# Attention with routed FFN on one core: routing and FFN steps given out by other waiting times of the builder's model, another order behind the last output, a two-chain last FFN, and more warming matmuls

## The chip, the cores and the metric

The kernel runs on one core of one Trainium2 chip. The core has a matrix engine (PE, with its weight loads PEld), three engines for element work (DVE, ACT and POOL) and a queue engine (SP) that issues most DMAs. The metric is device microseconds of one execution; lower is better. Matrix sums are built in eight PSUM banks.

## What is computed

There are 8 batches of 3136 tokens with 256 features. Per batch, the reference computes squared-ReLU attention without a softmax, multiplies by `u`, and then lets the 128 tokens with the highest gate scores pass through a small FFN:

```python
scores = (1 / S) * z @ z.T              # z: 3136 x 64
x = u * (relu(scores) ** 2 @ v)         # v, u: 3136 x 256
s = x @ w_gate
top = argpartition(-s, 128)[:128]       # per batch
y = relu(x[top] @ w1) @ w2              # 256 -> 1024 -> 256
x[top] += sigmoid(s[top])[:, None] * y
```

The matrix products must keep nearly float32 accuracy, so the kernel splits operands into a high and a low part and multiplies hi·hi, hi·lo and lo·hi.

## The kernel before, in words

**Tiling.** A batch is cut into six chunks of 512 tokens (0 to 5; chunk 5 is called `FIFTH`) and a rest of 64 tokens (`WHOLE`). For each chunk the kernel goes over key tiles, two of 128 tokens at a time. One such pair is a *slot*. A slot has four score matmuls (`sc`, PE), the squared ReLU with its high and low part (`a`, `hi`, `lo`: ACT, DVE, POOL), and twelve product matmuls that add to the banks `acc` (PE). Squares that another chunk has computed already come back turned from DRAM (`qk<-squares`). When a chunk is complete, DVE evicts it times `u` (`ut<-acc,ut`), turns it and stores it to the output; POOL and DVE form its gate scores.

**Routing.** `route(b)` finds the 128th-highest score of a batch by radix search: eight rounds in which DVE counts (`ge`, `cnt`), PE sums over partitions (`tot`) and DVE settles four more bits. Then come `cols`, `places` and four `find` steps (`ids`), an indirect DMA that gathers the chosen rows from the output (`xe<-out,ids`, POOL queue), and the FFN (`expert`): `turn` (`xeT`), `hidden` (`h`), `turn_h` (`hT`), `back` (`y`). An indirect DMA (`scatter`) writes the rows back.

**The last batch.** Its rows are ranked in a first step over chunks 0 to 2; chunks 3 and 4 are merged in one at a time (`merge`), and chunk 5 and the rest together at the very end (`last_merge`, `finish_last`, `finish_rest`). The FFNs of the two batches before it are put off (`put_off`, the list `held`) and given out in the last slots, as filler behind the last attention work. So behind the last output there are: scores of chunk 5 and of the rest, counting on DVE, `find`, the gather, the last FFN and its scatter.

**What sets the order.** The order of instructions on every engine is fixed when the kernel is built. The builder keeps its own clock (`Clock`: a cost for every instruction, a time for every tile). Work that is not PE work is a `job` with a rank; PE work is chosen in `choices`: score matmuls first (priority 0), then steps of chains (1), then products (2 or 3), among those that are ready by the builder's clock. A *chain* is a list of steps on different engines, each started when the one before is done; routing and FFN are chains. `step_when` says when a chain's PE step may be given out: at its operands' time by the builder's clock plus `MARGIN` = 0.3 for chains with a negative `lag`, plus `FAR` = 1.5 for all others. On the chip nothing of this clock exists: an engine takes its instructions in the order given, and waits for semaphores. Where an operand is later on the chip than by the builder's clock, PE stands still, with all that is behind that instruction.

All batches' routing goes through one chain, `far`; the turning of `u` for the rest (`uT`) goes through it too. The put-off FFNs are two chains with lag 20, the last FFN and the rank search at the end are a chain with lag -9, and the rest's scores (`spread<-own`) are a chain with lag 0.

Constants (identity, tokens, gate weights) are loaded in an early slot by `load_consts`; one POOL job, `use_consts`, turns them and gives DVE five instructions with them. `start` begins with ten matmuls on zeros (`warm`) before the first data are there.

In the profile nearly every instruction has line L198, that of a helper which notes it; instructions are told apart by the names of their tiles.

## Time and profile before

| what | before |
|---|---|
| time, median of 3 runs | 2173.46 us (2173.14 to 2174.82) |
| the profiled execution's own time | 2174.97 us |
| its span, first to last instruction | 2173.2 us |
| PE busy | 2114.3 us (97%) |
| DVE, ACT, POOL busy | 65%, 63%, 62% |
| mean granted TensorE clock | 0.989 |
| DMA | 428 MB, 197 GB/s |

The time lies 1.8 us over the span. Rows of the timeline read: start in us, duration in us, engine, line, operation, out<-in, count; in brackets the idle time of the engine just ahead, and what ended it. In a list of waits the numbers are us in total, times, and the longest. In a table of windows, `PEclk` is the clock that TensorE was granted in that stretch, as a share of full speed.

### The profile page before, as it was taken

The numbers are of one execution on the slowest core, as the hardware profiler recorded it, in microseconds if no ns is written. First come the engines' busy times: TensorE is split into PE (matmuls) and PEld (weight loads), VectorE is DVE, ScalarE is ACT, GpSimd is POOL, SyncE is SP. The second block draws the span as 40 slices with busy tenths as digits, with TensorE's granted clock in tenths as the row PEclk, the third lists the DMA queues.
The fourth block names the chain that finished last, engine by engine and source line by source line (L and its number), as shares of the span: only waits on it lengthen the run. The fifth ranks groups of instructions, "written<-read, shape, count | busy, mean of one in ns | idle before, by whom it ended". The sixth has DMA issues, their size and how long they took to land. (4 is left out here: it accounts for less than half of the span.)

```text
span 2173.2 us, 29259 instructions
## 1 busy us (share of the span) xinstructions
PE 2114.3 (97%) x9558; PEld 1704.6 (78%) x9558; DVE 1420.2 (65%) x2156; ACT 1361.9 (63%) x1583; POOL 1350.9 (62%) x634
## 2 busy tenths in 40 slices
PE   8999999999999999999999999999999999999997
PEld 6788877888778887788877888778887887778775
DVE  6765587545975459754686556955579664876773
ACT  7676576655766557655676556666576665876542
POOL 6466666567755677556765568565785566756551
PEclk9999999999999999999999999999999999999998
DMA  6688867777686866877668777687776677658741
GB/s 195 200 244 236 202 194 203 216 203 183 194 224 201 214 171 192 245 217 189 180 202 245 203 189 192 198 245 190 182 214 187 190 190 193 202 168 232 179 119 64
DMA packets 426121, 428.38 MB, mean 197 GB/s; under 512 B 129008, under 2 KB 329328, under 8 KB 422384
## 3 DMA queue, kind: packets, MB, share of 16 engines
q1 hardware_dynamic: 424624, 423.89, 71.2%
q0 software_dynamic: 768, 2.10, 0.3%
q8 instruction: 75, 1.23, 0.2%
q14 instruction: 78, 0.64, 0.1%
q10 hardware_dynamic: 576, 0.52, 0.1%
HBM read 238.44 MB, written 175.37 MB: 190 GB/s over the span
## 5 line engine op out<-in xcount | busy, mean ns | idle before, releaser
L198 PE MATMUL acc<-hi,V 128*128 128x512 f32 x4800 | 1235.8, 395 | 8.5 <-DVE ut L198 5.8
L198 PEld LDWEIGHTS acc<-hi,V 128*128 128x128 f32 x4800 | 895.0, 189 | 206.2 <-DVE ut L198 7.1
L198 POOL TENSOR_TENSOR lo<-a,hi 128x1024 fp32r<-128x1024 f32 (+1 forms) x231 | 550.1, 2384 | 391.9 <-ACT a L198 238.2
L198 PE MATMUL acc<-lo,V 128*128 128x512 f32 x2304 | 640.8, 395 | 1.5 <-POOL lo L198 1.4
L198 DVE STREAM_TRANSPOSE aT<-a 128x512 f32<-128x512 f32 (+2 forms) x622 | 379.4, 646 | 274.1 <-ACT a L198 217.9
L198 PEld LDWEIGHTS acc<-lo,V 128*128 128x128 f32 x2304 | 432.4, 189 | 101.0 <-issue 5.4
L198 POOL TENSOR_TENSOR lo<-qk,hi 128x1024 fp32r<-128x1024 f32 x161 | 406.9, 2528 | 158.1 <-ACT hi L198 137.3
L198 ACT ACTIVATE a<-sc 128x1024 f32<-128x1024 f32 (+1 forms) x392 | 353.4, 902 | 226.9 <-DVE aT L198 114.0
L198 ACT ACTIVATE hi<-a 128x1024 fp32r<-128x1024 f32 (+1 forms) x384 | 366.4, 955 | 188.6 <-PE acc L198 182.4
L198 ACT CAST hi<-qk 128x1024 fp32r<-128x1024 f32 x240 | 251.8, 1049 | 241.1 <-PE acc L198 202.8
L198 PE MATMUL sc<-Z,ZH 128*128 128x512 f32 (+1 forms) x728 | 278.1, 385 | 9.7 <-ACT a L198 5.7
L198 PE MATMUL sc<-Z,ZL 128*128 128x512 f32 (+1 forms) x728 | 276.3, 382 | 0.3 <-POOL ZL L198 0.3
L198 ACT ACTIVATE a<-a 128x1024 f32<-128x1024 f32 x247 | 262.0, 1061 | 7.3
L198 DVE TENSOR_TENSOR lo<-a,hi 128x1024 fp32r<-128x1024 f32 (+1 forms) x105 | 186.2, 1774 | 43.9 <-ACT a L198 32.9
L198 DVE TENSOR_TENSOR a<-sc,a 64x512 f32<-64x512 f32 (+3 forms) x145 | 118.3, 816 | 91.4 <-ACT hi L198 70.7
L198 PEld LDWEIGHTS sc<-Z,ZH 128*128 128x128 f32 x728 | 137.9, 189 | 42.0 <-ACT a L198 8.6
L198 POOL TENSOR_TENSOR ut<-x,w_run 128x1024 f32<-128x1024 f32 x45 | 125.7, 2793 | 65.9 <-DVE x L198 65.9
L198 PEld LDWEIGHTS sc<-Z,ZL 128*128 128x128 f32 x728 | 139.0, 191 | 31.3 <-POOL ZL L198 0.8
L198 DVE TENSOR_TENSOR lo<-qk,hi 128x1024 fp32r<-128x1024 f32 x79 | 134.9, 1707 | 25.4 <-ACT hi L198 25.3
L198 DVE SCALAR_TENSOR_TENSOR ut<-acc,ut 128x512 f32<-128x512 f32 x96 | 62.6, 680 | 87.8 <-PE acc L198 87.7
L198 POOL TENSOR_TENSOR V<-vst,V 128x512 fp32r<-128x512 f32 x62 | 98.8, 1609 | 16.4 <-ACT V L198 12.8
L198 POOL TENSOR_TENSOR lo<-own,hi 128x512 fp32r<-128x512 f32 x47 | 63.5, 1351 | 65.3 <-ACT hi L198 53.4
(170 smaller groups left out, 1183.4 us busy)
## 6 DMA issues: line engine op xcount, KB each, us to landing
squares<-aT SPq DMA_DIRECT2D x240, 512.0 KB, 4.4
qk<-squares SPq DMA_DIRECT2D x480, 256.0 KB, 6.1
ut<-in_ut SPq DMA_DIRECT2D x48, 512.0 KB, 5.1
vst<-in_v SPq DMA_DIRECT2D x188, 128.0 KB, 3.7
out<-x SPq DMA_DIRECT2D x188, 128.0 KB, 3.5
squares_own<-aT SPq DMA_DIRECT2D x47, 256.0 KB, 2.0
own<-squares_own SPq DMA_DIRECT2D x188, 64.0 KB, 2.4
zst<-in_zt SPq DMA_DIRECT2D x86, 128.0 KB, 6.5
```

Source lines behind the costliest of these rows:

```text
L198: got = real(*args, **kw)
```

## The change

- `FAR` is 4.0 instead of 1.5; chains with lag 1 (`far` in the last batch) have 2.0; the put-off FFNs (lag 20) have 0.3 and the lowest priority, 5, behind products. Consecutive PE steps of a chain no longer wait on each other. The builder counts a gather as done no earlier than 2.0 behind its DMA queue.
- The POOL job of the constants waits 2.0 (`SLACK`) longer by the builder's clock, and DVE's part becomes two jobs of their own (`weigh_consts`).
- In the last batch the tokens and split scores for `find` (`tokens`) are made ahead, no longer between ranking and `find`. The rest's chain has rank -1 and lag -7, and its product is always on DVE.
- The put-off FFNs are cut into steps of four matmuls; their last sum (`add`) and scatter wait until the last gather is issued.
- The last FFN is two chains, one for each half of the 1024 hidden features, with `back_half` in place of `back`; it takes `acc` banks (`paired`).
- `warm(22)` in place of `warm(10)`; behind the last gather, matmuls on a constant (356 columns) fill the times in which by the builder's clock PE has nothing to do for over 0.3.

```diff
-FAR = 1.5
+FAR = 4.0
...
-            end = begin + 3.5
+            end = max(begin + 3.0, self.queue + 2.0)
...
-        staged["consts"] = c_sb, st, w_run
-        job("pool", now[0] + 2, lambda e: use_consts(), [st, c_sb, w_run])
-    def use_consts():
-        c_sb, st, w_run = staged.pop("consts")
+        job("pool", now[0] + 2, lambda e: use_consts(c_sb, st), lambda: max(clock.after(x) for x in (st, c_sb)) + SLACK)
+        for h in range(NK):
+            job("dve", now[0] + 4, lambda e, h=h: weigh_consts(h, w_run), ok=lambda: "ident" in consts)
+    def use_consts(c_sb, st):
...
+        consts["all16"] = c16
...
-        w_col = const.tile([P, NK], F32, name="w_col")
-        w_row = const.tile([P, NK, P], F32, name="w_row")
-        for h in range(NK):
-            nc.vector.scalar_tensor_tensor(
-                w_row[:, h, :Q], w_run[:, h * Q : (h + 1) * Q], 1.0, consts["fold"],
-                op0=ALU.mult, op1=ALU.mult, accum_out=w_col[:, h : h + 1],
-            )
-            nc.vector.tensor_scalar(w_row[:, h, :], consts["ones"], w_col[:, h : h + 1], None, op0=ALU.mult)
-        consts["wg_row"] = w_row
-        place = const.tile([P, 1], F32, name="place")
-        nc.vector.tensor_reduce(place, consts["before"], axis=AX.X, op=ALU.add)
-        consts["place"] = place
...
+    def weigh_consts(h, w_run):
+        if h == 0:
+            consts["wg_col"] = const.tile([P, NK], F32, name="w_col")
+            consts["wg_row"] = const.tile([P, NK, P], F32, name="w_row")
+            consts["place"] = const.tile([P, 1], F32, name="place")
+            nc.vector.tensor_reduce(consts["place"], consts["before"], axis=AX.X, op=ALU.add)
+        w_row, w_col = consts["wg_row"][:, h], consts["wg_col"][:, h : h + 1]
+        nc.vector.scalar_tensor_tensor(
+            w_row[:, :Q], w_run[:, h * Q : (h + 1) * Q], 1.0, consts["fold"], op0=ALU.mult, op1=ALU.mult, accum_out=w_col
+        )
+        nc.vector.tensor_scalar(w_row, consts["ones"], w_col, None, op0=ALU.mult)
...
-        rank = k + 1
+        rank = k + 1 if scored else -1
...
         def lower(e):
...
         def total(e):
...
-            job("pool|dve", rank + 2, product, [st["s"]], took=takes(D), ok=lambda: b in turned_u)
+            job("pool|dve" if scored else "dve", rank + 2, product, [st["s"]], took=takes(D), ok=lambda: b in turned_u)
...
         def product(e):
...
-                chain_of([("dve", column), ("pe", [spread]), ("act", seen)], 0)
+                chain_of([("dve", column, (), (), lambda: end["merge"]["ready"]()), ("pe", [spread]), ("act", seen)], -7)
...
-            [("pe", [lambda h=h: spread(h) for h in range(NK)], (), (), have), ("act", seen), ("dve", look), ("dve", m["old"])]
+            [("pe", [lambda h=h: spread(h) for h in range(NK)], (), (), have), ("act", seen, (), (), lambda: m["ready"]()), ("dve", look), ("dve", m["old"])]
...
         def start():
...
+            if late:
+                chain_of([("dve", st["tokens"])], 4)
...
-        def begin():
-            tok = consts["tok16"][:R].rearrange("p (t w) -> p t w", w=2)
-            if scored:
-                what = moe.tile([TP, NT, 5], BF16, name="what", tag="what")[:R]
-                nc.vector.tensor_copy(what[:, :, :2], tok)
-                cut(st["G"], what[:, :, 2:])
-                st["what"] = what
-            else:
-                st["what"] = tok
-            pick(0)
-        steps = [("dve", begin), ("dve", lambda: pick(1))]
+        def tokens():
+            what = moe.tile([TP, NT, 5], BF16, name="what", tag="what")[:R]
+            nc.vector.tensor_copy(what[:, :, :2], consts["tok16"][:R].rearrange("p (t w) -> p t w", w=2))
+            cut(st["G"], what[:, :, 2:])
+            st["what"] = what
+        if scored:
+            st["tokens"] = tokens
+        else:
+            st["what"] = consts["tok16"][:R].rearrange("p (t w) -> p t w", w=2)
+        steps = [("dve", lambda: pick(0)), ("dve", lambda: pick(1))]
...
-            "row": lambda: m["row"], "col": lambda: m["col"], "old": lambda: old(0), "new": new,
+            "ready": lambda: "row" in m, "row": lambda: m["row"], "col": lambda: m["col"], "old": lambda: old(0), "new": new,
...
+        def tokens():
...
-            st["what"] = what
+            cnt["what"] = what
...
         def find():
...
-                nc.tensor.matmul(st["ps"][:, :w], st["oh5"][:T4, i], st["what"][:, i], start=i == 0, stop=False)
+                nc.tensor.matmul(st["ps"][:, :w], st["oh5"][:T4, i], cnt["what"][:, i], start=i == 0, stop=False)
...
         def kept():
...
-            ("pe", [spread_old], (), (), lambda: (b, c) in looked),
+            ("pe", [spread_old], (), (), lambda: (b, c) in looked), ("dve", tokens),
...
-            ("dve", pick), ("pe", [find]), ("dve", kept),
+            ("dve", pick), ("pe", [find], lambda: [cnt["what"]]), ("dve", kept),
...
+            if merged(b):
+                end["gathered"] = True
...
         def weigh():
...
+        def paired(name):
+            return b == B - 2 or (name == "h" and b < B - 1)
         def bank(name, e):
...
-            if name == "h" or b == B - 2:
+            if paired(name):
...
-            if name == "h" or b == B - 2:
+            if paired(name):
...
         def rings_of(name, e):
-            return (sc_ring,) if roomy and e == 0 and (name == "h" or b == B - 2) else ()
+            return (sc_ring,) if roomy and e == 0 and paired(name) else ()
...
         def room(name):
-            if roomy and name != "h" and b != B - 2:
+            if roomy and not paired(name):
...
-        def scatter():
-            y = moe.tile([P, D], F32, name="y", tag="big", bufs=2)
+        def back_half(e, j):
+            if e == j == 0:
+                st["ps"] = bank("y", 0)
+            f = 4 * e + j % 4
+            w2h, w2l = (w[:, :W].rearrange("p (f d) -> p f d", d=D) for w in (ZH, ZL))
+            h, w = (("hh", w2h), ("hh", w2l), ("hl", w2h))[j // 4]
+            nc.tensor.matmul(
+                st["ps"][:m, :D], st[h, e][:, f % 4, :], w[:, f, :], start=e == j == 0, stop=(e, j) == (1, 11)
+            )
+            if (e, j) == (0, 11):
+                st["half"] = True
+        def add():
+            st["y"] = y = moe.tile([P, D], F32, name="y", tag="big", bufs=2)
...
+        def scatter():
...
-                outs[b], bass.IndirectOffsetOnAxis(ap=st["ids"][:m, :], axis=0), y[:m], None
+                outs[b], bass.IndirectOffsetOnAxis(ap=st["ids"][:m, :], axis=0), st["y"][:m], None
...
         def weights():
...
-        upper = ("pe", y[: 2 * NF], weights, rings_of("y", 0), room("y"))
...
+        after = lambda: "gathered" in end
...
-            return first, hid(0) + hid(1) + tur(0) + tur(1) + [upper], dif(0) + dif(1) + [("pe", y[2 * NF :]), ("dve", scatter)]
+            fours = lambda ops: [("pe", ops[i : i + 4]) for i in range(0, len(ops), 4)]
+            begin = ("pe", y[:4], weights, rings_of("y", 0), room("y"))
+            if b != B - 2:
+                back_steps = [begin, *fours(y[4 : 2 * NF]), *dif(0), *dif(1), *fours(y[2 * NF :])]
+            else:
+                back_steps = [*dif(0), *dif(1), begin, *fours(y[4:])]
+            return first, hid(0) + hid(1) + tur(0) + tur(1), back_steps + [("dve", add, (), (), after), ("pool", scatter)]
...
-            return first, hid(0) + hid(1), tur(0) + dif(0) + tur(1) + dif(1) + [whole, ("dve", scatter)]
-        return first, [], hid(0) + tur(0) + dif(0) + hid(1) + [("sp", lambda: bring_weight(2))] + tur(1) + dif(1) + [whole, ("dve", scatter)]
+            half = lambda e: [lambda j=j: back_half(e, j) for j in range(12)]
+            down = lambda e: ("act", lambda: (high(e), low(e)), (), (hi_ring, lo_ring) if e == 0 else (), lambda: e == 0 or ("hh", 0) in st)
+            ups = [[lambda i=i, e=e: hidden(e, i) for i in range(3 * NK)] for e in range(2)]
+            flips = [[lambda f=f, e=e: turn_h(e, f) for f in range(4)] for e in range(2)]
+            one = [
+                ("pe", ups[0], lambda: w_here, (), room("h")), ("act", lambda: rectify(0), (), (a_ring,)),
+                ("pe", flips[0], (), (), room("hT")), down(0),
+                ("pe", half(0), weights, (), room("y")),
+            ]
+            two = [
+                ("pe", ups[1], lambda: [*w_here, st["xl"]], (), lambda: ("h", 0) in st and room("h")()),
+                ("act", lambda: rectify(1), (), (), lambda: ("hr", 0) in st),
+                ("pe", flips[1], (), (), lambda: ("hT", 0) in st and room("hT")()), down(1),
+                ("pe", half(1), weights, (), lambda: "half" in st), ("dve", add), ("pool", scatter),
+            ]
+            one.insert(0, ("pe", [lambda: chain_of(two, -8)]))
+            return first, one, []
+        return first, [], hid(0) + tur(0) + dif(0) + hid(1) + [("sp", lambda: bring_weight(2))] + tur(1) + dif(1) + [whole, ("dve", add), ("pool", scatter)]
...
     def start():
-        warm(10)
+        warm(22)
...
-        late = MARGIN if x.lag < 0 else FAR
+        late = MARGIN if x.lag < 0 or x.lag == 20 else 2.0 if x.lag == 1 else FAR
...
     def choices():
...
-                    got.append((t, 1 + (x.lag if x.lag < 0 else 0) * 0.01, ("step", x)))
+                    got.append((t, 5 if x.lag == 20 else 1 + (x.lag if x.lag < 0 else 0) * 0.01, ("step", x)))
...
-            x.ready = max(x.ready, clock.mark)
+            if not x.steps or x.steps[0][0] != "pe":
+                x.ready = max(x.ready, clock.mark)
...
+        if "gathered" in end and bank_when() is not None and min([x[0] for x in got], default=t + 1.0) > t + 0.3:
+            bank = take_bank("idle")
+            c16 = consts["all16"]
+            nc.tensor.matmul(bank[:, : cst16.shape[1]], c16[:, :P], c16, start=True, stop=True)
+            drop_bank(bank)
+            lost = 0.0
+            continue
```

More of the change, by code (lines that the diff above doesn't have):

```diff
@@ L1763, in weigh @@
             gate_of(st["xe"][:m], ge[:m])
-            g = moe.tile([P, 1], F32, name="g", tag="g", bufs=2)
+            g = moe.tile([P, 1], F32, name="g", tag="g", bufs=3)
             nc.scalar.activation(g[:m], ge[:m], AF.Sigmoid)
@@ L1982, in start @@
     def start():
-        warm(10)
+        warm(22)
         stage_z(0, 0, uses=1)
-        first = moe.tile([P, 1], F32, name="g", tag="g", bufs=2)
+        first = moe.tile([P, 1], F32, name="g", tag="g", bufs=3)
         nc.scalar.activation(first, idle[0][:, :1], AF.Sigmoid)
```

## The prediction

> **What bounds the kernel now.** I read the page's busy times first, then PE's list of waits, then windows cut where the granted clock changes, then the timeline around the longest waits and behind the last output.
>
> ```profile
> span 2173.2 us, 29259 instructions
> ...
> PE 2114.3 (97%) x9558; PEld 1704.6 (78%) x9558; DVE 1420.2 (65%) x2156; ACT 1361.9 (63%) x1583; POOL 1350.9 (62%) x634
> ```
>
> PE is the bound: the others stand at 62 to 65%. It stands still for only 58.9 us (2173.2 - 2114.3), so all that can be won without less PE work is there, and in stretches in which a wait has halved its clock. In PE's list of waits stand us in total, times, and the longest:
>
> ```profile
> PE xeT L198 <- DMA xe<-out,ids: 11.7, 6, 5.7
> PE acc L198 <- DVE ut L198: 5.8, 3, 4.3
> PE sc L198 <- ACT a L198: 5.7, 6, 1.4
> PE cols L198 <- DVE mk L198: 5.6, 6, 1.0
> PE tot L198 <- DVE cnt L198: 3.7, 7, 1.0
> PE ids L198 <- DVE what L198: 3.5, 1, 3.5
> ...
> PE y L198 <- DMA wl<-w2l_there: 2.1, 3, 0.8
> ```
>
> ```profile
> 7.60:17.80 10.20, 7.60 (x16) 5.24 (x17) 6.77 (x5) 7.97 (x11) 7.61 (x6) 0.50 0.73 196
> 69.00:75.85 6.85, 5.46 (x13) 4.31 (x14) 6.37 (x15) 3.14 (x3) 0.79 (x2) 0.50 0.20 76
> 376.20:379.60 3.40, 3.40 (x9) 2.68 (x9) 3.40 (x7) 3.37 (x5) 1.48 (x1) 0.50 0.13 29
> 645.90:649.30 3.40, 3.40 (x10) 2.63 (x9) 3.20 (x5) 3.29 (x5) 1.15 (x1) 0.50 0.99 202
> 2103.40:2110.20 6.80, 5.37 (x17) 4.24 (x17) 3.88 (x15) 1.14 (x2) 0.46 (x1) 0.50 0.92 203
> 2151.20:2164.80 13.60, 7.55 (x20) 5.15 (x21) 0.86 (x3) 1.86 (x5) 2.27 (x3) 0.50 0.09 29
> ```
>
> Windows start, length, busy times, and third from the end the granted clock: 0.50 in all six. Ahead of the second to fifth stands one wait each (for `ut`, twice for a gather, for `what`); such a stretch costs half its length, 3.4, 1.7, 1.7 and 3.4 us.
>
> **Waits ahead of the last output.** Nearly all waits listed are of chain steps that PE was given too early by the builder's clock. Given out 2.5 us later (`FAR` 4.0 for 1.5), a step waits 2.5 less, and PE does products in that time; the cover is the steady stream of products, and nothing else is needed of it.
>
> ```profile
> 368.27 1.15 POOL L198 DMA_INDIRECT xe<-out,ids  x1 [0.17 <-issue]
> 375.31 0.41 PE L198 MATMUL xeT<-c_sb,xe 128*128 128x128 f32 x2 [2.25 <-DMA xe<-out,ids]
> 645.33 0.44 PE L198 MATMUL xeT<-c_sb,xe 128*128 128x128 f32 x2 [1.92 <-DMA xe<-out,ids]
> ```
>
> *Gathers.* Five waits of 11.7 - 5.7 = 6.0 us (longest 2.25) and two half-clock stretches (1.7 + 1.7): 9.4. Later by 2.5 they vanish, the 2.25 narrowly; I take 9.0. If the margin helps half as much, 4.
> *Radix search.* `cols` and `tot`, 5.6 + 3.7, none over 1.0, so less than the 2.5: 9.0; half, 4, at least.
> *Weights* (`y`): 2.0 of 2.1, or 0.
>
> ```profile
> 2101.59 2.30 DVE L198 COPY what<-c 128x8 bf16<-128x8 bf16 x1
> ```
>
> *Tokens of the merge.* A copy of 8 columns took 2.30 us, while POOL's `lo` ran; PE stood 3.5 us behind it and lost 3.4 to the clock. The same six DVE instructions now come ahead of the ranking, and `find` is given out 2.0 behind them. DVE does the same work, its blocked copy now delays a count. Gain 6.5 of 6.9; 3 if only the clock stretch goes.
>
> ```profile
> 64.55 2.41 DVE L198 TENSOR_SCALAR w_row<-c_sb,w_col 128x128 f32<-128x128 f32 x1
> ...
> 66.89 2.32 DVE L198 SCALAR_TENSOR_TENSOR w_row<-w_run,c_sb 128x32 f32<-128x32 f32 x1
> ...
> 70.39 3.35 PE L198 MATMUL acc<-hi,V 128*128 128x512 f32 x7 [4.29 <-DVE ut L198]
> ```
>
> *Constants.* Five DVE instructions are one block; two of them took 2.3 to 2.4 us beside POOL's `lo`, and the eviction that frees PE's bank stood behind: 4.3 us plus 3.4 of half clock, 7.7. In two jobs of lower urgency than the eviction (by the code rank `now` + 4 = 15, against the chunk's last slot, 12), DVE can evict between them. I take 6.5. From below: one blocked pair (2.4) still ahead of the eviction, and a further stretch, would leave 0; a loss of 2.4 if one more pair is caught.
> The Trainium skill (SBUF — State Buffer, Who interferes with whom) says that DVE instructions with two SBUF inputs, or in a two-port mode, and POOL instructions exclude each other for a whole instruction, and that issue order decides who waits. That speaks against this part: cut in two, the block meets POOL as often, and by that rule alone the gain would be 0 rather than 6.5. The three rows of 2.3 to 2.4 us agree with the rule; the order on DVE decides.
>
> Together 9.0 + 9.0 + 2.0 + 6.5 + 6.5 = 33.0, bounds 4 + 4 + 0 + 3 - 2.4 = 8.6 and 35.4. What is late next is what PE waits for without a chain (`sc<-a` 5.7, which stays); some of what is won will be found there. I count 85%: 28.
>
> **The start.** Twelve more matmuls of zeros: the first score matmul waits for data, up to where the first window above begins, and in that window PE idles another 2.6 us (10.2 - 7.6) for ACT's first results. The stretch 7.60 to 17.80 may lose at most half of PE's 7.6 busy us, and more likely nothing, since ACT feeds PE there (7.97 of 10.2 busy): 0, from -2 to +0.5.
> The Trainium skill (TensorE: Matmul & The Clock Gate, What's actually happening) says that the clock halves after an idle window of about 3.4 us, with free-running windows, and rises after a busy one. By it the extra matmuls hold the clock to the next gap and no longer, which is the 0 above; with no second gap they would give 3.8. A wait of 1.92 us at 645 was enough here for a half-clock stretch, so the trace is stricter than the page's whole idle window.
>
> **Behind the last output.**
>
> ```profile
> 2126.72 1.04 PE L198 MATMUL turned<-c_sb,ut 128*128 128x128 f32 x8
> ...
> 2134.30 0.34 DVE L198 SCALAR_TENSOR_TENSOR beats<-row,col,c_sb 128x128 bf16<-128x128 f32 x1
> ...
> 2138.77 1.42 PE L198 MATMUL acc<-V,rest_hl 128*128 128x512 f32 x5
> ...
> 2143.26 0.25 DVE L198 TENSOR_SCALAR own<-c_sb,col 64x64 f32<-64x64 f32 x1
> ...
> 2145.56 0.43 PE L198 MATMUL spread<-own,c_sb 64*128 64x64 f32 x2
> ...
> 2150.47 1.03 POOL L198 DMA_INDIRECT out<-y,ids  x1 [7.71 <-DVE y L198]
> ...
> 2153.10 0.98 POOL L198 DMA_INDIRECT xe<-out,ids  x1 [0.30 <-issue]
> ...
> 2156.04 0.66 PE L198 MATMUL xeT<-c_sb,xe 128*128 128x128 f32 x2 [5.72 <-DMA xe<-out,ids]
> ...
> 2168.50 0.48 DVE L198 SCALAR_TENSOR_TENSOR y<-y,g,xe 128x256 f32<-128x256 f32 x1 [1.88 <-PE y L198]
> ```
>
> DVE has counted chunk 5 by 2134.6, but the rest's scores come 11 us later: its products end at 2140.2, because put-off FFN steps (priority 1) go ahead of products (2); and `spread` starts 2.0 us behind its operand (2143.5), behind PE's put-off `y` matmuls. With priority 5 for the put-off steps, the 24 rest products follow the last chunk's turning, which ends at 2127.8, without a break: 24 x 0.234 = 5.6 us (two take 0.47 below), so 2133.4, 6.8 earlier. With `spread` at once, 8.8 earlier; but DVE then does the rest's sums (four of about 0.42) amid its counts, so I take 8. The gather stood behind two scatters that now follow it (2150.47 to 2153.10): 2.1 more, 10 in all. The put-off PE work (per FFN 6 x 0.47 for `h`; by their columns 24 x 0.12 for `y` and a little over 1 for the turning, about 7) fills PE from 2133 to the gather's landing, about 2146, and what is left over has the lowest priority; its adds and scatters lie beside the last FFN.
>
> ```profile
> 2131.70 0.63 PE L198 MATMUL lent<-wh,xh 128*128 128x512 f32 x2
> ...
> 2132.17 0.64 PE L198 MATMUL lent<-wl,xh 128*128 128x512 f32 x2
> ...
> 2158.18 1.05 PE L198 MATMUL lent<-wl,xh 128*128 128x512 f32 x2
> ...
> 2159.03 1.05 PE L198 MATMUL lent<-wh,xl 128*128 128x512 f32 x2
> 2160.19 0.60 ACT L198 ACTIVATE hr<-lent 128x512 f32<-128x512 f32 x1 [3.08 <-PE lent L198]
> ```
>
> The last FFN took 12.5 us from `xeT` to its sum, at half clock: two matmuls 0.85 apart instead of 0.47. With PE kept busy by put-off and warming matmuls and in two halves: `xeT` (half of 0.66) and `xh` (256 columns, half of 0.60) with their hand-overs 0.9; `h` of half 0, 1.4; ReLU 0.6 and half 1's `h` beside it; `hT` 0.6, `hh` 0.6 (as the ReLU row); then half 1's ReLU, `hT`, `hh` (1.9, PE meanwhile on half 0's `y`), and its 12 `y` matmuls, 1.4; with 0.6 of hand-overs 8.0. Gain 4.5. Sum 14.5; PE steps that are 0.3 late by design and the warming matmuls' overshoot take some: 12.5. Bounds: 4 (the scatters' 2.1 and half of 4.5), 17 (all, and DVE's sums for free).
>
> **Sum.** 28 + 12.5 + 0 = 40.5; the profiled execution took 2174.97 (1.8 over its span), so 2134.5. The median of the runs is 1.5 lower: **2133**. Bounds: 8.6 + 4 - 0.5 = 12.1, so 2161; 35.4 + 17 + 2 = 54.4, so 2119.
>
> **Rivals.**
> *The waits move.* PE is so near full that each wait saved comes back at `sc<-a` or `acc`, as DVE's and POOL's blocked instructions stay. For it: rows of 2.3 to 2.4 us anywhere on DVE. Against: the others' 35% of slack. Ahead of the last output only the lower bound, 8, then 12.5: 2153.
> *The end stays long.* The builder's clock misjudges the hand-overs there, PE waits in order on put-off or half-FFN steps and falls to half clock again: 28, but 4: 2141.
> *Slower: the last batch's routing comes too late.*
>
> ```profile
> 1956.56 0.38 PE L198 MATMUL uT<-c_sb,ur 128*64 128x128 f32 x2
> ...
> 2003.30 1.17 DVE L198 TENSOR_REDUCE gate<-ut 128x16 f32<-128x1024 f32 x1
> ...
> 2111.11 0.27 ACT L198 COPY row<-old 128x128 f32<-128x128 f32 x1 [1.55 <-PE old L198]
> ...
> 2126.92 0.59 ACT L198 COPY row<-spread 128x512 f32<-128x512 f32 x1 [2.36 <-PE spread L198]
> ```
>
> The one chain `far` must end batch 6's routing and `uT` before batch 7's can begin. Its 17 PE steps (`gate`, 8 `tot`, `cols`, `places`, 4 `ids`, `xeT`, `uT`) each come 2.5 later: `uT` at 1956.6 + 42.5 = 1999, still 4 us ahead of the scores at 2003. From there 15 steps at +0.5 make 7.5, of which the tokens give back over 2; and from `row<-old` at 2111.4 to its use at 2126.9 there are 15.5. So I expect it hidden. Each step that comes late by more than that pushes the gather one for one; it takes 15.5 + 40.5 = 56 us before the kernel is slower than now, say 2180.
> *It does nothing.* The builder's clock is off by more than 4 at the same places and the end is as long: 2173.
>
> **Chances.** Forecast 0.64, with its own range 2122 to 2146; the waits move 0.13; the end stays long 0.13; slower 0.06; nothing 0.04. A difference of 0.2% (4.3 us) is about what can be told here. Faster 0.90, same 0.04, slower 0.06. The range, 2119 to 2158, takes in the bound above, both rivals on the fast side, and leaves out the last two.
>
> **What would show it.** PE's waits for `xeT`, `cols`, `tot`, `what` and the 4.3 for `ut` gone, the granted clock 1.0 from 18 to the last output; rest products without put-off steps between them; the gather ahead of both put-off scatters; two `h` matmuls 0.47 apart in the last FFN, 8 us from `xeT` to the sum. I am wrong if PE's idle time ahead of the last output stays over 25 us, or if `row<-old` comes behind the last chunk's `row<-spread`.

## The result and the profile after

The changed kernel takes **2124.82 us** (median of 4, 2123.40 to 2126.41) where the kernel before takes 2174.14 beside it: ratio 0.977, 95% interval 0.9753 to 0.9787, so 49 us faster. The forecast was 2133, with its own range 2122 to 2146. Its profiled span is 2122.7 us.

The page of the changed kernel, its span and the engines' busy times:

```profile
span 2122.7 us, 29280 instructions
...
PE 2099.1 (99%) x9575; PEld 1698.0 (80%) x9575; DVE 1409.9 (66%) x2147; ACT 1368.3 (64%) x1591; POOL 1352.4 (64%) x635
```

PE's idle time went from 58.9 to 23.6 us (2122.7 - 2099.1), and its busy time fell by 15.2, for the most part the half-clock stretches that are gone: the granted clock is 1.00 from 17.4 us to the end. Windows of the changed kernel (start, length, PE busy, and third from the end the granted clock), and the middle one of the kernel before:

```profile
0.00:54.33 54.33, 48.28 (x187) 34.73 (x188) 35.09 (x37) 39.74 (x50) 34.40 (x23) 0.97 0.67 197
54.33:2080.00 2025.67, 2014.15 (x9178) 1634.07 (x9178) 1352.18 (x2027) 1317.05 (x1517) 1307.87 (x606) 1.00 0.74 204
2080.00:2122.70 42.70, 36.64 (x213) 29.19 (x211) 22.59 (x85) 11.47 (x25) 10.09 (x8) 1.00 0.23 82
```

```profile
54.33:2120.00 2065.67, 2029.41 (x9188) 1640.33 (x9187) 1365.27 (x2044) 1310.63 (x1510) 1308.06 (x604) 1.00 0.73 201
```

Between the start and the last chunk PE stands still 11.5 us instead of 36.3, and what is left in PE's list of waits there is the attention's own:

```profile
PE sc L198 <- ACT a L198: 8.6, 7, 2.1
PE sc L198 <- DVE a L198: 0.8, 2, 0.5
PE acc L198 <- DVE ut L198: 0.7, 1, 0.7
PE sc L198 <- DMA Z<-ZL: 0.7, 1, 0.7
PE acc L198 <- POOL rest_hl L198: 0.5, 1, 0.5
```

No wait for `xeT`, `cols`, `tot`, `what` or `wl` is in it. What moved there instead: `sc<-a` on ACT grew from 5.7 to 8.6, and the waits for DVE's `a` (0.8) and for `ZL` (0.7) are new, 4.4 us together.

**Where the 50.5 us of the two spans lie.** Both kernels do the same 7104 products of chunks 0 to 5 in nearly the same order, so the time of the n-th of them, before less after, shows where time was won. The last of them ends each attention; its rows before and after:

```profile
2123.70 0.61 PE L198 MATMUL acc<-lo,V 128*128 128x512 f32 x2
```

```profile
2084.46 0.62 PE L198 MATMUL acc<-lo,V 128*128 128x512 f32 x2
```

```
product   before    after   won so far   won since the row above
    0       14.3     14.1       0.3
  148       64.1     64.0       0.1       -0.1   start
  296      115.4    108.2       7.2        7.1   constants
 1776      546.2    532.0      14.1        7.0   batch 0's routing, its FFN
 2664      812.9    793.8      19.1        4.9   batch 1's
 5920     1777.4   1747.4      29.9       10.9   batches 2 to 5
 6956     2078.5   2045.5      33.0        3.1   batch 6's, the last batch's first steps
 7103     2123.9   2084.7      39.2        6.2   merge of chunk 4
```

So 39.2 us were won ahead of the last product, and 50.46 - 39.24 = 11.2 behind it. Behind it the changed kernel's timeline reads:

```profile
2088.36 0.39 PE L198 MATMUL old<-diag,c_sb 128*128 128x128 f32 x2
...
2089.62 0.31 ACT L198 COPY row<-old 128x128 f32<-128x128 f32 x1
2089.78 0.64 ACT L198 COPY row<-spread 128x512 f32<-128x512 f32 x1
...
2090.45 0.29 DVE L198 SCALAR_TENSOR_TENSOR own<-spread,c_sb 128x128 f32<-128x128 f32 x1 [4.54 <-ACT row L198]
...
2092.36 2.12 PE L198 MATMUL acc<-V,rest_hl 128*128 128x512 f32 x8 [0.17 <-POOL rest_hl L198]
...
2096.80 0.42 DVE L198 TENSOR_SCALAR xr<-acc 64x256 f32<-64x256 f32 x1
...
2099.36 0.43 PE L198 MATMUL spread<-own,c_sb 64*128 64x64 f32 x2 [0.69 <-DVE own L198]
...
2103.66 0.36 PE L198 MATMUL ids<-c,oh 128*128 128x2 bf16 x5 [0.97 <-DVE oh L198]
...
2104.59 0.99 POOL L198 DMA_INDIRECT xe<-out,ids  x1 [12.29 <-DVE ids L198]
...
2107.68 0.41 DVE L198 SCALAR_TENSOR_TENSOR junk<-xe,w_bc 128x256 f32<-128x256 f32 x1
...
2108.40 0.38 PE L198 MATMUL xeT<-c_sb,xe 128*128 128x128 f32 x2
...
2110.05 0.63 PE L198 MATMUL h<-wh,xh 128*128 128x512 f32 x2
2110.51 0.63 PE L198 MATMUL h<-wl,xh 128*128 128x512 f32 x2
...
2117.85 0.69 PE L198 MATMUL idle<-c 128*128 128x356 bf16 x3
2118.05 0.48 DVE L198 SCALAR_TENSOR_TENSOR y<-y,g,xe 128x256 f32<-128x256 f32 x1 [1.95 <-PE y L198]
```

The rest's products follow the turning with one break of 0.17 us and end at 2094.48; the gather is ahead of both put-off scatters; two `h` pairs stand 0.46 apart, full clock. This part is read as us behind the end of the last product of chunk 5 (2124.31 and 2085.07). In the two traces of the changed kernel it agrees to 0.01 us, while the part ahead of it moves by several us from execution to execution. So the experiments are compared by this table, made from the same rows of each trace. Marks are starts (of the second matmul where there are two), but for the last product, the rest's products and the end of the span, which are ends:

```
                 before changed FAR1.5  FAR6 tokens own-ch no-fill  prio  scatter gather best
last product ends 2124.3 2085.1 2107.5 2093.8 2092.2 2090.5 2088.6 2089.4 2086.2 2091.6 2093.3
rest products      15.9    9.4    8.7   16.4    8.8    8.8    9.4   16.6    9.4    9.4    8.8
old row's matmul  -13.5    3.4   -1.7   13.6   -7.1   -2.6    3.4    3.4    3.4    3.4   -5.3
spread of the rest 21.4   14.5   13.0   23.5   13.0   13.1   14.5   20.9   14.4   14.4   13.0
gather             28.8   19.5   18.2   29.1   18.2   18.3   19.5   26.0   19.5   19.5   18.2
xeT                32.0   23.4   22.1   32.5   22.2   22.2   23.4   29.7   23.4   23.9   22.2
last sum           44.2   33.0   31.7   41.7   31.7   31.7   32.3   38.9   33.0   33.4   31.0
end of the span    48.9   37.6   36.3   46.4   36.4   36.4   36.9   43.6   37.6   38.1   35.6
```

The last 148 products (from 6956 on, "the last slots") can be compared from trace to trace too: in five traces of kernels in which nothing was changed there, they took 0.2 to 0.5 us longer than in the first trace of the changed kernel.

### The profile page after: what moved, and what is told of

The parts are those of the page before. It is cut to its first block, busy times and chain, and to the rows that moved or that the text cites. A ratio compares the mean times of both kernels' runs of the same rounds, so it can differ in the third digit from the quotient of the medians.

```text
span 2122.7 us, 29280 instructions
## 1 busy us (share of the span) xinstructions
PE 2099.1 (99%) x9575; PEld 1698.0 (80%) x9575; DVE 1409.9 (66%) x2147; ACT 1368.3 (64%) x1591; POOL 1352.4 (64%) x635
## 4 chain that ended last, share of the span: by engine, by line
PE 81%; DVE 6%; DMA 4%; issue 3%; ACT 2%; POOL 2%; SPq 2%; POOLq 0%; DVEq 0%; ACTq 0%
PE acc L198 67%; PE sc L198 12%; DVE aT L198 2%; SPq L198 2%; DVE V L198 1%; ACT a L198 1%; DMA squares<-aT 1%; DMA vst<-in_v 1%; ACT hi L198 1%; POOL V L198 1%; PE y L198 1%; DVE beats L198 1%; PE h L198 1%; POOL lo L198 1%; DVE lo L198 1%
## 5 line engine op out<-in xcount | busy, mean ns | idle before, releaser
L198 POOL TENSOR_TENSOR lo<-a,hi 128x1024 fp32r<-128x1024 f32 (+1 forms) x237 | 574.4, 2425 | 416.9 <-ACT a L198 296.5
L198 POOL TENSOR_TENSOR lo<-qk,hi 128x1024 fp32r<-128x1024 f32 x155 | 385.0, 2484 | 161.6 <-ACT hi L198 126.4
L198 ACT ACTIVATE a<-a 128x1024 f32<-128x1024 f32 x255 | 270.6, 1061 | 7.4
L198 DVE TENSOR_TENSOR lo<-a,hi 128x1024 fp32r<-128x1024 f32 (+1 forms) x99 | 150.8, 1523 | 34.4 <-ACT a L198 24.4
L198 PEld LDWEIGHTS sc<-Z,ZH 128*128 128x128 f32 x728 | 137.1, 188 | 43.8 <-ACT a L198 12.5
L198 DVE TENSOR_TENSOR a<-sc,a 64x512 f32<-64x512 f32 (+3 forms) x137 | 108.2, 790 | 85.8 <-ACT hi L198 74.1
L198 DVE TENSOR_TENSOR lo<-qk,hi 128x1024 fp32r<-128x1024 f32 x85 | 147.8, 1738 | 25.3 <-ACT hi L198 19.3
L198 POOL TENSOR_TENSOR ut<-x,w_run 128x1024 f32<-128x1024 f32 x45 | 131.7, 2927 | 32.7 <-DVE x L198 32.5
L198 DVE TENSOR_TENSOR V<-vst,V 128x512 fp32r<-128x512 f32 (+1 forms) x41 | 63.1, 1539 | 46.2 <-ACT V L198 42.5
```

The costliest lines, as they stand in the source:

```text
L198: got = real(*args, **kw)
```

## The experiments

My theory: the waits ahead of the last output came from steps given out too early and go with `FAR`; behind it, the order of rest products and put-off steps and the clock set the time. Runs of one group share a chip and the runs of the kernel before, whose median was 2175.58, 2179.70 and 2178.68 us in the three groups; so the changed kernel's 0.977 would be about 2125.5 on the first chip and 2129.6 on the second, and on the third it was run again.

### FAR back at 1.5

```diff
-FAR = 4.0
+FAR = 1.5
```

> The changed kernel with FAR back at 1.5, the gather's cost in the builder's clock left as changed. Theory (later give-out removes PE's waits for cols, tot, xeT and the weights): 15 to 26 us slower than the changed kernel, so 2140 to 2151, with cols and tot waits of about 9 us back in PE's list and at least one half-clock stretch behind a gather. Rival (the gather's new cost, not FAR, removed the long waits): the xeT waits stay gone and only cols and tot come back, 9 to 12 us slower, so 2134 to 2137.

Measured: 2148.87 us (2145.63 to 2152.02), some 23 slower; in the trace the last product is 22.4 us later. From its list of PE's waits:

```profile
PE tot L198 <- DVE cnt L198: 6.0, 9, 1.3
PE cols L198 <- DVE mk L198: 5.6, 6, 1.0
...
PE y L198 <- DMA wl<-w2l_there: 1.2, 4, 0.5
```

The waits of the radix search are back: `cols` with 5.6 us as before, `tot` with 6.0 where 3.7 stood. The waits for `xeT` are not, and with them stay away the half-clock stretches at the gathers: those the gather's new cost in the builder's clock removes by itself. So the theory's size was right and one of its signs was not: half-clock came back only in the last slots, where 7.4 of the 22.4 us were lost, beside waits for `ut` and `lo` of 2.3 and 2.1 us. What put these there I did not separate; without them the loss is 15.0, the low end of what was expected.

### FAR at 6.0

```diff
-FAR = 4.0
+FAR = 6.0
```

> The changed kernel with FAR at 6.0. Theory of the forecast's slower rival (batch 6's routing and uT, 17 PE steps, must end before the last batch's routing can begin): uT comes 34 us later, the first gate fold of the last batch is late by 25 to 35 us, the old rows come behind the last chunk's row, and the kernel is 15 to 35 us slower, 2140 to 2160. Rival (that chain has slack or the builder's order gives way): within 3 us of 2125.

Measured: 2139.38 us (2136.01 to 2142.03), some 14 slower, just under the 15 to 35 expected. The rows of the gate scores and of the old row (instructions, then first and last start):

```profile
L198 DVE TENSOR_REDUCE gate<-ut x45: 1167/1206/1221, 77.7 to 1978.5; 128x16 f32<-128x1024 f32 x45
...
L198 PE MATMUL gate<-c_sb,gate x16: 190/220/248, 290.2 to 1998.8; 128*98 128x32 f32 x14, 128*48 128x32 f32 x2
...
L198 PE MATMUL old<-diag,c_sb x6: 270/273/275, 2063.5 to 2107.4; 128*128 128x128 f32 x6
```

The last batch's scores are summed at 1978.5, but its first routing step comes at 1998.8, 20 us later, because `uT` of the same chain starts only at 1995.6. (In the changed kernel: 1971.4, 1975.4, and `uT` at 1962.2.) The old row is then 13.6 us behind the last product, the end 8.7 us longer. So the forecast's slower rival is a real mechanism, with its place and sign; `uT` begins to hold up the last batch between 4.0 and 6.0. The other 8.7 us lie ahead of the last product, most of them around 1227 us, where PE waits 2.9 us for DVE's `hi` and has half the clock for 6.8 us; that is another cause, and why `hi` is late there I did not separate.

### The constants as before

```diff
-        job("pool", now[0] + 2, lambda e: use_consts(c_sb, st), ... + SLACK)
-        for h in range(NK):
-            job("dve", now[0] + 4, lambda e, h=h: weigh_consts(h, w_run), ...)
+        job("pool", now[0] + 2, lambda e: use_consts(), [st, c_sb, w_run])
```

> The changed kernel with the constants' work undone (one block in the POOL job, as before). Theory (order on DVE decides): the 4.3 us wait for ut and the half-clock stretch behind it come back at 66 to 76 us, 7 us slower, 2132. Rival (the later waits absorb it): under 3 us slower.

Measured: 2132.20 us (2131.79 to 2134.07), some 7 slower, and 7.0 at the last product. Its timeline has the old picture again, a blocked DVE instruction and PE behind it:

```profile
66.49 2.33 DVE L198 SCALAR_TENSOR_TENSOR w_row<-w_run,c_sb 128x32 f32<-128x32 f32 x1
...
70.00 2.50 PE L198 MATMUL acc<-hi,V 128*128 128x512 f32 x5 [4.28 <-DVE ut L198]
```

In the changed kernel the eviction goes first, and the constants then meet no POOL work at all:

```profile
64.19 1.28 DVE L198 SCALAR_TENSOR_TENSOR ut<-acc,ut 128x512 f32<-128x512 f32 x2
...
69.53 0.17 DVE L198 SCALAR_TENSOR_TENSOR w_row<-w_run,c_sb 128x32 f32<-128x32 f32 x1
...
69.75 0.29 DVE L198 TENSOR_SCALAR w_row<-c_sb,w_col 128x128 f32<-128x128 f32 x1
```

The seven us hold through two thousand: nothing later absorbs them.

### The merge's tokens between ranking and find

```diff
-            ("pe", [spread_old], (), (), lambda: (b, c) in looked), ("dve", tokens),
+            ("pe", [spread_old], (), (), lambda: (b, c) in looked),
...
-            ("dve", pick), ("pe", [find], lambda: [cnt["what"]]), ("dve", kept),
+            ("dve", lambda: (pick(), tokens())), ("pe", [find]), ("dve", kept),
```

> The changed kernel with the merge's tokens put back between ranking and find. Theory (the 6.2 us that the two traces differ by between 2078 and 2124 come from the tokens): the wait for what and the half-clock stretch come back, 5 to 7 us slower, 2130 to 2132. Rival (find's give-out 2.0 behind its operands instead of 1.5 is enough): within 2 us. A third way: tokens ahead of the counts made the last batch's old row late by some 2 us (they took 5.2 us there, from 2064.9 to 2070.1), and without them the end is 2 us shorter, which would offset part of it: 3 to 5 us slower.

Measured: 2130.27 us (2129.20 to 2130.52), some 5 slower. In the last slots 4.7 us are lost, to this wait and a half-clock stretch of 3.4 us behind it:

```profile
2057.59 2.30 DVE L198 TENSOR_TENSOR less<-less,what 128x4 f32<-128x4 f32 x1
...
2060.15 0.24 PE L198 MATMUL ids<-what,oh 128*128 128x5 bf16 x4 [2.26 <-DVE what L198]
```

Another 2.4 us lie further ahead, where the edit does not reach: 1.5 of them at a half-clock stretch at 567 us, and about 0.9 late in the run, which nearly every other trace shows against the first one too. And the end is 1.3 us *shorter* (36.4 for 37.6), because the old row's matmul now stands 7.1 us ahead of the last product instead of 3.4 behind it. So the third way was right: the tokens ahead of the ranking won some 4.7 and cost 1.3.

### The merge's tokens in a chain of their own

```diff
-            ("pe", [spread_old], (), (), lambda: (b, c) in looked), ("dve", tokens),
+            ("pe", [spread_old, lambda: chain_of([("dve", tokens)], 4)], (), (), lambda: (b, c) in looked),
...
-            ("dve", pick), ("pe", [find], lambda: [cnt["what"]]), ("dve", kept),
+            ("dve", pick), ("pe", [find], lambda: [cnt["what"]], (), lambda: "what" in cnt), ("dve", kept),
```

> The changed kernel with the merges' tokens as a chain of their own beside the ranking, not ahead of it. Theory (ahead of the ranking they delayed the old row, which came 2 us behind the last chunk's scores): the old row is out before the last chunk's row is wanted, the end is 1 to 2 us shorter, 2123 to 2124. Rival (the same DVE instructions, blocked by POOL as often, delay the counts all the same): within 0.7 us of the changed kernel.

Measured: 2129.19 us (2128.86 to 2131.79), ratio to the kernel before 0.9776 (0.9758 to 0.9795): no difference that can be measured. In the trace the end is 1.3 us shorter, as the theory says; but in the last slots 5.2 us are lost, as the rival says, and more:

```profile
2066.76 2.24 DVE L198 TENSOR_TENSOR less<-col,what 128x4 f32<-128x4 f32 x1
...
2071.41 2.31 DVE L198 TENSOR_TENSOR less<-less,what 128x4 f32<-128x4 f32 x1
...
2084.86 0.26 PE L198 MATMUL ids<-what,oh 128*128 128x5 bf16 x4 [2.10 <-DVE oh L198]
```

Three of the instructions on four columns take 2.2 to 2.3 us here beside POOL; now they stand among the counts, and `find` waits 2.1 us for the ranking. Another 2.4 us are a wait for `ut` at 2049.7 with a half-clock stretch behind it, while DVE counts and makes the tokens of the earlier merge. A net loss of 3.9 us in one trace is within the spread of single executions on this chip (2125.75 to 2130.68 for one kernel below), so the medians can't settle what it is worth.

### Without the filling matmuls, and ten at the start

```diff
-        if "gathered" in end and bank_when() is not None and ...
-            ...
...
-        warm(22)
+        warm(10)
```

> The changed kernel without the matmuls that fill PE's idle time behind the last gather, and with 10 instead of 22 warming matmuls at the start. Theory (put-off steps fill PE there, and the trace has only five filling matmuls, the granted clock 1.0 to the end; at the start the clock falls again in the next gap): within 1 us of 2125. Rival (the fillers keep the clock): half clock behind the gather again, 2 to 3 us slower, 2127 to 2128.

Measured: 2128.12 us (2127.29 to 2129.79), ratio 0.977 (0.9752 to 0.9788): the same. The end is 0.7 us shorter: the five fillers of the changed kernel stood in PE's way, and behind the last product the granted clock stays 1.00 without them until after the last sum. At the start, twelve matmuls less change nothing:

```profile
7.61 0.76 PE L198 MATMUL sc<-Z,ZH 128*128 128x512 f32 x1 [1.97 <-DVE Z L198]
...
14.06 0.79 PE L198 MATMUL acc<-hi,V 128*128 128x512 f32 x1 [2.06 <-ACT hi L198]
```

The first product starts at 14.1 us in both.

### The put-off steps at priority 1

```diff
-                    got.append((t, 5 if x.lag == 20 else 1 + ...
+                    got.append((t, 1 + ...
```

> The changed kernel with the put-off FFN steps at priority 1 instead of 5, so ahead of products; 0.3 us margin kept. Theory (rest products late because put-off steps went ahead of them): the rest's products end 5 to 7 us later after the last chunk's products, the gather 4 to 7 us later, 2129 to 2132. Rival (DVE's counting sets the gather; put-off work done early leaves less to be done in the last FFN): within 2 us.

Measured: 2135.71 us (2130.31 to 2138.11), 7.4 slower than the next kernel, which shares its chip and, as shown below, stands for the changed kernel there. From the last product on it takes 5.9 us longer:

```profile
2105.04 0.95 PE L198 MATMUL acc<-V,rest_hl 128*128 128x512 f32 x3
...
2115.39 0.98 POOL L198 DMA_INDIRECT xe<-out,ids  x1 [18.75 <-DVE ids L198]
```

The rest's products end 7.2 us later behind the last product, the gather starts 6.5 later. The theory holds; with the put-off work done early, half a us comes back between the gather and the last sum.

### Scatters free to come before the gather

```diff
-        after = lambda: "gathered" in end
+        after = lambda: True
```

> The changed kernel with the put-off FFNs' adds and scatters free to come ahead of the last gather. Theory (each scatter ahead of the gather holds it by 1.1 us on POOL): only one or none is ready by then, as the put-off y steps now come last, so 0 to 1.2 us slower, up to 2126. Rival (both are given out ahead by the builder's clock): 2 us or more slower, 2127 and over.

Measured: 2128.32 us (2125.75 to 2130.68), and every mark of the table as in the changed kernel. With the put-off steps last, no scatter is ready ahead of the gather: the gate does nothing by itself. In the run before this one, with priority 1 and the gate, the scatters start 1.3 and 2.6 us behind the gather: either edit alone keeps them behind it.

### The last FFN as one chain

```diff
+            return first, hid(0) + hid(1), tur(0) + dif(0) + tur(1) + dif(1) + [whole, ("dve", add), ("pool", scatter)]
...
-            return b == B - 2 or (name == "h" and b < B - 1)
+            return b == B - 2 or name == "h"
```

> The changed kernel with the last FFN as one chain again: both halves' h, then turning, then the y matmuls of both, h in the score banks. Theory (at full clock most of the last FFN's 12.5 us was the clock; the split only lets ACT and PE overlap): from xeT to the sum 1 to 2 us longer than the changed kernel's 9.6, so 1 to 2 us slower in all. Rival (the split gave the gain): 3 us or more slower.

Measured: 2131.49 us, the median of five runs from 2130.13 to 2132.49, against 2127.02 (2125.37 to 2129.54) of the changed kernel on the same chip: 4.5 slower, ratios 0.9786 (0.9769 to 0.9802) and 0.9765 (0.9748 to 0.9782). The intervals of the two ratios overlap, but the slowest of the five runs of the changed kernel is faster than the fastest of these five. Its one profiled execution was disturbed (5847 us), so the times of its rows can't be read. The medians are on the rival's side (3 us or more), that the split gave the gain; but the edit also brings 30 fillers behind the gather in place of 5, and those 5 cost 0.7 us above; no trace shows where the time went. So the split's own share is not shown.

### The gather's old cost in the builder's clock

```diff
-            end = max(begin + 3.0, self.queue + 2.0)
+            end = begin + 3.5
```

> The changed kernel with the gather's old cost in the builder's clock (done 3.5 behind its begin), FAR at 4.0. Theory (FAR and the gather's cost each suffice for the gathers' waits, the longest of which was 2.25 before and FAR gives 2.5): no xeT wait over 0.5 us ahead of the last output, within 1.5 us of the changed kernel. Rival (the queue term is what holds them): xeT waits of 2 us or more in the first batches with half-clock stretches, 4 us or more slower.

Measured: 2130.29 us (2128.32 to 2133.00), 3.3 over the changed kernel on that chip, ratio 0.978 (0.9762 to 0.9797). PE's only wait for a gather in the whole trace is the last one:

```profile
PE xeT L198 <- DMA xe<-out,ids: 0.9, 1, 0.9
```

No wait for `xeT` ahead of the last output and no half-clock stretch behind a gather: `FAR` at 4.0 covers the gathers as well. As far as these waits go, each of the two edits is enough. The 3.3 us lie between theory and rival, and the last product is only 1.8 later than in the changed kernel's trace there; whether anything of it belongs to the edit stays open.

### No fillers, and the last batch's routing at 1.5

```diff
-        late = MARGIN if x.lag < 0 or x.lag == 20 else 2.0 if x.lag == 1 else FAR
+        late = MARGIN if x.lag < 0 or x.lag == 20 else 1.5 if x.lag == 1 else FAR
```

Beside this, the two edits of the run without fillers.

> The changed kernel without the filling matmuls behind the last gather, 10 warming matmuls, and 1.5 instead of 2.0 for the one routing chain in the last batch. Theory (the old row came 2 us too late, worth 1.26 us of the end, and the fillers cost 0.7): some 20 steps at 0.5 bring it 10 us earlier; from the last product to the end 35.6 instead of 37.6, 2 us faster than the changed kernel on the same chip. Rival (0.5 less brings back a wait for cols, tot or what, with a half-clock stretch): 0 to 5 us slower ahead of the last product, the end still shorter.

Measured: 2128.85 us (2127.50 to 2132.50), 1.8 over the changed kernel on that chip; not faster. The end is 35.6 us as forecast, 2.0 shorter. But ahead of it:

```profile
2080.28 2.58 DVE L198 SCALAR_TENSOR_TENSOR oh<-rk,c_sb 128x640 bf16<-128x640 f32 x1
...
2082.91 0.26 PE L198 MATMUL ids<-what,oh 128*128 128x5 bf16 x4 [2.61 <-DVE oh L198]
```

`oh` takes 0.82 us alone and 2.58 here. In the first trace of the changed kernel it took 3.05, and `find`, given out later, did not wait for it; at 1.5 `find` no longer clears it. 4.4 us are lost in the last slots, with a half-clock stretch. The rival's way, with its size.

### The changed kernel again

> The changed kernel itself, as the measure for the three others of this chip: 0.977 of the kernel before, and from the last product to the end 37.6 us.

Measured: 2127.02 us (2125.37 to 2129.54), 0.9765 (0.9748 to 0.9782), the end 37.64 us as in its first trace. Its last product ends at 2089.8, 4.7 later than in the first trace of the same instructions, in steps of about one us spread over the batches; what makes them I did not separate. No version tried is measurably faster.

## Why the prediction was right, point by point

**The sign and the kind: right.** PE was the bound, and its waits were the gain. Undone alone, the parts cost: `FAR` 22.4 us at the last product (15.0 without the last slots), the constants 7.0, the tokens 4.7 less 1.3, the priority 5.9 behind the last product. The rest chain's new rank and lag, its product on DVE and the cutting of the put-off FFNs into fours were not undone alone.

**The size ahead of the last output: too small.** 28 was forecast, 39.2 won. The measured time is 8 us under the forecast, near the lower end of its range, and all of that is here. The step that failed is "I count 85%": 5 us were taken off the full sum of 33.0 for waits that come back elsewhere. 4.4 us did come back, and yet more than 33.0 was won, so the terms themselves were too small. This is not the chance of one trace: by the medians 49.3 us were won, and 51.7 in the third group, less 11.2 behind the last product. Of the 39.2, 25.9 us (7.0 + 4.9 + 10.9 + 3.1 in the table) came from gathers, radix search and weights, where 9.0 + 9.0 + 2.0 = 20 were counted. The list of waits measures from PE's modelled ends. In batches 2 to 4, where the listed waits of chain steps make 2.3 to 2.5 us each, 2.8, 3.1 and 3.7 were won. With `FAR` alone undone, 15.0 of the 25.9 were lost again, where that trace's list has 12.8 us (`tot`, `cols`, `y`): the list is short there too. Why the difference of nearly 6 us in all is not in the list, no run separates.

**Constants:** 6.5 of at most 7.7 forecast, 7.1 won. The rule of the Trainium skill (SBUF — State Buffer, Who interferes with whom) did not cost the gain: the cut block met POOL nowhere (0.17 and 0.29 us per instruction), and the order on DVE decided. Where the rule did bite was the tokens: 2.38 and 2.23 us for two of the six instructions in the changed kernel too.

**Tokens:** 6.5 forecast, 6.2 won in the last slots. "DVE does the same work, its blocked copy now delays a count" was there, but not priced: the delayed counts made the old row late, 1.3 us of the end, as both runs that moved the tokens show.

**Gathers:** right that the waits go, for half the reason: `FAR` and the gather's cost each do it alone.

**The start:** 0, as forecast. With 22 warming matmuls the first score matmul starts at 8.71 instead of 7.65 and the first product at 14.1 instead of 14.3; with ten, at 14.1 as well.

**Behind the last output:** 12.5 forecast, 11.2 won. Rest products 6.5 earlier behind the last product (6.8 forecast), `spread` 7.0 (8 forecast after DVE's share), gather 9.3 (10). The last FFN took 9.65 us from `xeT` to the sum (2108.40 to 2118.05), not 8.0, so 2.8 was won, not 4.5. Put-off `y` matmuls stood ahead of `h`, which began 1.65 us behind `xeT` (2110.05) where 0.9 was forecast, and the fillers cost 0.7: that is 1.45 of the 1.65 us. The "put-off and warming matmuls" that were to keep PE busy had the wrong weights: the put-off ones did it alone.

**The scatters' gate** was credited with 2.1 us; undone alone it costs nothing, since the priority has the same effect.

**The slower rival** did not happen, but its slack was misjudged. `uT` stayed 9.2 us ahead of the last batch's scores (1962.2 and 1971.4), where 4 was forecast. From the first routing step of the last batch to the old row took 113.0 us (1975.4 to 2088.4), for 104.7 before (2005.95 to 2110.7): 8.3 more, where 7.5 less 2 were forecast. The slack of 15.5 us, however, was read off the slow kernel: from the last gate sum to the last product passed 121.0 us before and 113.7 after, because PE itself no longer stood still there. 15.5 less 7.3, 8.3 and 1.4 (a later first step) is 1.5 below zero, and the old row came late. The sign I had given for this, `row<-old` behind the last chunk's row, could not have shown it: the change itself gives out the last chunk's row only behind the old one, and it came 0.16 us after it.

## What to carry to other kernels

Where one engine is nearly full and takes its instructions in a fixed order, a step that depends on slow side work should be given out well behind the time at which its operands are expected: in the runs here a microsecond of waiting there was lost whole, and a longer wait could cost the clock besides. The margin has an upper end, which is where the side chain's own last step becomes late: for this kernel 1.5 was too early, 6.0 too late. Slack that is read from a slow trace shrinks by what the change itself wins.

## What the runs showed of the hardware that I had not expected

DVE instructions on four to eight columns, 0.16 to 0.18 us alone, took 2.2 to 2.4 us beside a POOL subtraction of 2.4 us, some of them in every trace that can be read and wherever they were moved (2064.90 to 2067.2 and 2067.38 to 2069.6 in the changed kernel). Moving them does not cure it by itself; they have to run while POOL does not. For the earlier merge, at 2039.1 to 2040.2 in the same trace, the same six instructions met no POOL work and took 0.16 to 0.18 us each.

Whether a wait costs the clock is not a matter of its length alone: 1.92 us at 645 in the kernel before brought a half-clock stretch, while the changed kernel's longest wait ahead of the last output, 2.08 us, brought none. The traces show what else counts. In each trace but the disturbed one, all changes of the granted clock lie on one grid with steps of 3.413 us: in the changed kernel at 14.01, 17.42 and 2123.45, which are 1 and 617 steps apart. The changed kernel and the run with the tokens between ranking and `find` have the same instructions up to the last batch and the same wait of 2.08 us near 566 us. In the latter it lies inside one step of the grid; in the changed kernel the end of a step cuts it into 1.26 and 0.82. First the run with the tokens moved, then the changed kernel: the row behind the wait, and two steps of the grid as windows:

```profile
567.35 0.80 PE L198 MATMUL sc<-Z,ZH 128*128 128x512 f32 x1 [2.08 <-ACT a L198]
...
563.94:567.35 3.41, 1.33 (x7) 0.76 (x5) 3.31 (x10) 2.68 (x5) 0.90 (x1) 1.00 0.52 183
567.35:570.76 3.41, 3.41 (x8) 2.73 (x9) 2.17 (x4) 2.57 (x3) 2.77 (x3) 0.50 0.63 202
```

```profile
567.79 0.50 PE L198 MATMUL sc<-Z,ZH 128*128 128x512 f32 x1 [2.08 <-ACT a L198]
...
563.56:566.97 3.41, 2.15 (x10) 1.45 (x8) 3.31 (x11) 1.89 (x4) 0.08 (x1) 1.00 0.25 91
566.97:570.39 3.42, 2.60 (x11) 2.17 (x12) 2.17 (x4) 3.36 (x4) 2.79 (x3) 1.00 0.79 261
```

In three more traces the end of a step cuts the same wait of 2.08 us, and no stretch follows in them either. So the same instructions can gain or lose a stretch, 1.7 us, by where their waits fall on the grid. A sharp limit for the idle time in a step does not come out of the traces: 1.92 us brought a stretch in the kernel before, 1.83 and 1.88 brought none in the second trace of the changed kernel, but 1.64 did at 2062.4 in the run with the tokens moved. The Trainium skill (TensorE: Matmul & The Clock Gate, What's actually happening) has free-running windows of about 3.4 us, by which the place of a wait in its window would matter; the grid of 3.413 us and the two waits agree with that.

The same program, instruction for instruction, ended its last product 4.7 us later in its second trace than in its first, while the 37.64 us behind it agreed to a hundredth.
